# Keys times values of two pairs of heads in one slice, transposes apart from their loads, and another order of the first product's seven outer products

## The chip, the cores and the metric

One core of one Trainium2 chip runs the kernel. The metric is the time on the device in microseconds of one execution; smaller is better. PE is TensorE (the matrix engine), DVE is VectorE, ACT is ScalarE, POOL is GpSimd, SP is SyncE, whose queue issues nearly all DMAs here.

## What is computed

```python
kv  = einsum('bhsd,bhse->bhde', k, v)          # 8 batches, 8 heads, 576 rows, head size 64
out = einsum('bhsd,bhde->bhse', q, kv)         # linear attention, no softmax
rms = sqrt(mean(out * out, axis=-1, keepdims=True) + 1e-06)
x   = (out / rms * g_norm), heads side by side # 4608 rows x 512
h   = x @ w_in                                 # 512 -> 2048
g   = maximum(h, 0.0) ** 2
y   = g @ w_out                                # 2048 -> 512
```

All of it is in float32.

## The kernel before

The 4608 rows of x are 36 tiles of 128 rows, and four tiles make a strip: nine strips, numbered 0 to 8. A batch has 576 rows, four and a half tiles; the halves of two batches share a tile, so an even batch brings four tiles of its own, an odd one five, the first of them the shared one ("rest").

**The strips.** Each strip has an up part (x times `w_in`, then relu and square) and a down part (times `w_out`). Both use fast matrix multiplication: seven products of sums of blocks instead of eight of blocks. Strip 0 has an ordinary up part and one level in its down part; strip 1 has one level up and two levels down; strips 2 to 8 have two levels in both, 49 small products in each part. In those strips the up part is a list of 55 slots. `UP_SETS` orders the seven outer products ("sets", numbered 1 to 7): the set at place n issues its seven small products at slots 7n, 7n+2, ... 7n+12, so neighbouring sets alternate. Each small product is eight recorded matmuls. Three PSUM banks A, B and C serve a set. Bank A takes the inner products 1, 6, 7 and 4 one after another: each is added onto what lies there, so its former content is first copied to a `snap` tile (L1088 by ACT, or L1083 by DVE with an addition), and PE waits for that read. Bank B does so for 5 and 3.

**Where the sets' results go.** `UP_TO` names for each set the quarter of g that it writes and the quarter that it is added to: 11, 12, 21 and 22. Set 5 updates two quarters, and sends six of its additions to POOL (L1083). Four sets finish a quarter (`FINAL`): for these, relu and square run on ACT, in place (L1023, L1024), two or four slots after the product. DVE then makes the sums that the down part needs (`leaf_sums`, `add_s1`).

**POOL's sums.** The sets multiply `w_in` by four sums of x (`sum_x` 5, 6, 7 and 4) and by the inner sums of each set (`leaf_x`). POOL makes them at slots given by `SUM_AT` and by `at == 2`; those of the first set come at the end of the down part before (L966).

**Attention as slices.** Attention for the next strip is a list of slices that is worked off between the slots: `attend` spreads a strip's slices evenly over the first 42% of its weighted steps, so that they end near slot 46. Their kinds, in the order of a batch b from 2 on: for each of four pairs of heads `key_value` (20 recorded matmuls, two small copies on ACT, then the loads of keys and values two pairs ahead) and `transposed_query` (a DVE transpose, then the loads of queries two pairs ahead, four DMAs); after these, for each two tiles, `query` (64 recorded matmuls, squares on ACT), `mean_roots` (means on DVE, square root on ACT), `normalized` (reciprocal, a Newton step and a product on DVE), `squares_x` (DVE transposes), `send_x` (a store) and, later, `fetch_x` (four loads that turn the tile into x transposed). Keys, values and queries have two buffers each. Batches 0 and 1 use PE for the transposes (`features`, L527) instead of the store and loads. In strip 0 the slices follow a formula of their own (L1195 to L1197).

Each engine works through its instructions in the order written; the order is written by hand.

Of the kernel before, what the change touches and what calls it, by code (L numbers as in the profile page):

```python
# [10 lines left out]
FP32 = mybir.dt.float32  # L11
# [9 lines left out]
def kernel(  # L21
# [285 lines left out]
    ident = const.tile([P, P], FP32, name="ident")  # L307
    make_identity(nc, ident)

    kv_all = const.tile([P, 2 * NP + 1, P], FP32, name="kv_all")  # L310
    nc.gpsimd.memset(kv_all, 0.0)
    nc.vector.memset(k_rest, 0.0)
    nc.vector.memset(v_rest, 0.0)
# [26 lines left out]
    def keep_busy(ps, n):  # L340


        for _ in range(n):
            nc.tensor.matmul(ps, lhsT=ident, rhs=ident[:, : ps.shape[1]], start=True, stop=True)
# [25 lines left out]
            nc.tensor.transpose(ps[:, p], flat(q_rest[b // 2][:, 2 * p : 2 * p + 2]), ident)  # L370
        nc.scalar.copy(open_rest(b), ps)

    def key_value(b, p):
        tk, tv = main.pop(("k", b, p)), main.pop(("v", b, p))

        ps = apsum.tile([P, D], FP32, name="kv_ps", tag="at")
        if (b, p) == (0, 0):
            keep_busy(ps, 3)
        for c in range(C + 1):
            for h in range(2):  # L380
                a, w = (tk[:, h, c, :], tv[:, h, c, :]) if c < C else (k_rest[:, 2 * p + h], v_rest[:, b % 2, 2 * p + h])
                nc.tensor.matmul(ps[ts(h, D)], lhsT=a, rhs=w, start=c == 0, stop=c == C)  # L382
        d = kv_all[:, (NP * b + p) % (2 * NP + 1)]
        nc.scalar.copy(d[0:D, 0:D], ps[0:D])
        nc.scalar.copy(d[D:P, D:P], ps[D:P])
        kvd[b, p] = d
        if b < 2:
            if b == 1 and p < 2:
                load_next()
        else:  # L390
            load_next(names="kv")
            if p == NP - 1 and b + 1 < B:
                load_rest(b + 1, nc.sync)

    by_head = lambda t: t.rearrange("p (h d) -> p h d", d=D)

# [49 lines left out]

    queried = []

    def query(ns):
        ps = products_x(ns)  # L450
        parts = [ps[:, :, i] for i in range(len(ns))]
        queried.append((parts, squared_parts(parts)))

    def mean_roots(ns):
        parts, sqs = queried.pop()
# [135 lines left out]
    for b in range(1, B):  # L591
        for p in range(NP):
            pair = [(transposed_query, (b, p)), (key_value, (b, p))]
            slices += pair if b < Q_ON_PE else pair[::-1]
            fetch(1)
            if (b, p) == (X_ON_PE, 0):
                slices += late
        if b % 2 and b < Q_ON_PE:
            slices.append((rest_queries, (b,)))
        first_n = b // 2 * PAIR + (C if b % 2 else 0)  # L600
        ns = list(range(first_n, first_n + C + b % 2))
        for i in range(0, len(ns), 2):
            pair = ns[i : i + 2]
            slices += [(query, (pair,)), (mean_roots, (pair,))]
            fetch(1)
            slices.append((normalized, (pair,)))
            fetch(1)
            for n in pair:
                if b < X_ON_PE and i == C:

                    late = [(features, (n,))]
                    continue
                slices.append((features if b < X_ON_PE else squares_x, (n,)))
                if b < X_ON_PE and n % NT == NT - 1:
                    ready[n // NT] = len(slices)
            if b >= X_ON_PE:
                slices += [(send_x, (n,)) for n in pair]
                fetches.extend(pair)
    fetch(2)
    slice_at = [0]  # L620

# [119 lines left out]
    for p, t in zip((1, 2, 5), w_first):  # L741
        w_blk[0, p] = t.rearrange("p f (h e) -> p h f e", h=2)
    DEEP_ORDER = (4, 1, 2, 6, 5, 7, 3)
    UP_SETS = (1, 2, 6, 7, 5, 3, 4)
    to_stream = [(s, p) for s in range(DEEP) for p in ORDER if (s, p) not in w_blk]
    for s in range(DEEP, N_STRIP):
        to_stream += [("in", s, p) for p in UP_SETS if s >= DEEP_UP]
# [172 lines left out]
    def down_deep(s, k, i):  # L920
        p = DEEP_ORDER[k]
        if s == N_STRIP - 1 and k == 6 and i == 1:

            steps = together(s, p)
            for js in ((1,), (2, 6, 5, 7), (4, 3)):
                small_products(s, p, js)
                next(steps)
            return
        if k == 0 and s >= DEEP_UP:
            if i == 0:  # L930
                return
            for j in (7, 5, 6, 3):
                small_products(s, p, (j,))
                if first_sums_g:
                    first_sums_g.pop(0)()
            stream(2)
            leaf_sums(s, DEEP_ORDER[1])
            for slot in sorted(relus):
                relu_squares(slot)
            for slot in sorted(first_s):  # L940
                add_s1(s, slot)
            return
        if k == 6 and i == 1:
            small_products(s, p, (4,))
            return
        if s < N_STRIP - 1 or k < 6:
            small_products(s, p, ((1, 2, 3), (4, 5, 6, 7))[i])
        stream()
        q11, q12, q21, q22 = (gq[s, q] for q in (11, 12, 21, 22))
        if i == 1:  # L950
            if k == 3:
                minus(nc.vector, q22, q22, q11)
            if k == 4:
                minus(nc.vector, q21, q21, q11)
            if k == 6:
                deque(together(s, p), 0)
            return
        if k == 2:
            minus(nc.vector, q11, q12, q11)
        if k == 3:  # L960
            leaf_sums(s, DEEP_ORDER[k + 1])
        if k:
            deque(together(s, DEEP_ORDER[k - 1]), 0)
        if k < 6 and k != 3:
            leaf_sums(s, DEEP_ORDER[k + 1])
        if k == 6 and s + 1 < N_STRIP:  # L966
            leaf_x(s + 1, 0)


    first_s = {}  # L970
# [52 lines left out]
            nc.scalar.activation(o, o, AF.Relu)  # L1023
            nc.scalar.activation(o, o, AF.Square)  # L1024

    SUM_AT = {2: 5, 4: 6, 11: 7, 18: 4}
    FINAL = (2, 5, 3, 4)
    UP_TO = {1: (12, None), 2: (11, 12), 6: (12, 12), 7: (21, 12), 5: (22, 21), 3: (12, 12), 4: (21, 21)}
    up_bank = {}

    def up_slot(s, slot):

        for n, p in enumerate(UP_SETS):
            i, odd = divmod(slot - 7 * n, 2)
            if not odd and 0 <= i < 7:
                up_small(s, n, p, ORDER[i], slot)
        if slot in SUM_AT:
            sum_x(s, SUM_AT[slot])
        n, at = divmod(slot, 7)
        if at == 2 and n < 6:  # L1040
            leaf_x(s, n + 1)
        if s == DEEP_UP and at == 0 and n < 7:
            deep_differences_in(A_IN[UP_SETS[n]])
        relu_squares(slot)
        add_s1(s, slot)
        if slot in (1, 3, 5):
            small_products(s - 1, 3, ((slot + 9) // 2,))
        if slot == 5:
            stream()
            deque(together(s - 1, 3), 0)  # L1050
        if slot == 45:
            first_sums_g[:] = leaf_sums(s, 4, (3, 1, 2, 4))
        if slot in (49, 51, 53):
            small_products(s, 4, ({49: 1, 51: 2, 53: 4}[slot],))
        if slot in (46, 48, 50, 52):
            first_sums_g.pop(0)()

    def up_small(s, n, p, j, slot):
# [62 lines left out]
    for s in range(N_STRIP):  # L1121
# [21 lines left out]
        for i, (w, fn, a) in enumerate(steps):  # L1143
# [87 lines left out]
```

## Time and profile before

| | us |
|---|---|
| five runs: median (lowest to highest) | 968.47 (958.34 to 972.83) |
| the profiled execution | 968.47 |
| its span | 966.7 |
| mean granted PE clock | 0.974 |

Where the strips lie in the span: strip 0 down from about 95 to 164 us, strip 1 up to 230 and down to about 273. Then, for strips 2 to 8, the up part: 273 to 332, 372 to 434, 475 to 535, 575 to 637, 677 to 742, 782 to 832, 872 to 921. What lies between is the down part, about 40 us each, and the last one ends at 966.

A group in the profile is a source line, an engine, an operation and its tiles (`out<-in`); "idle before" is the time that an engine stood before such an instruction, and the arrow names what released it. Matmul ends are modelled, so a busy PE may still run slowly; the granted clock shows that.

The units of the sums below, in mean ns of one instruction: relu 627 and square 631 (128x512), `snap` copy on ACT 583, POOL's addition for set 5 1328, DVE's stream transpose 701, the small ACT copies of `key_value` (64x64) 203 and 207, squares of one tile on ACT 593.

### The profile page before, as it was taken

The page shows a single profiled execution, that of the slowest core. Times are in us where ns is not written, and L with a number is a line of the kernel's source. Part 1 is how long each engine was busy: PE and PEld are TensorE (multiplying, and loading weights), DVE is VectorE, ACT ScalarE, POOL GpSimd, SP SyncE. Part 2 cuts the span into 40 slices and gives each one's busy share as a digit, 9 for nine tenths or more (in the row PEclk, how much of TensorE's full clock was granted, in tenths as well). Part 3 has the DMA queues.
Part 4 walks back from the last instruction along what each step waited for, and adds up shares of the span by engine and source line. Part 5 has one row for each costly group of instructions (what it writes and reads, how often), then busy time and mean ns, then how long its engine had stood idle before and what let it go on. Part 6 is the DMA issues. An engine that isn't in the chain of part 4 may idle for free.

```text
span 966.7 us, 20798 instructions
## 1 busy us (share of the span) xinstructions
PE 902.7 (93%) x8246; PEld 838.2 (87%) x8246; DVE 755.2 (78%) x1289; ACT 323.2 (33%) x662; POOL 265.5 (27%) x287
## 2 busy tenths in 40 slices
PE   6999779899999899889998999889988999999997
PEld 6434668679999899889997999889988999999997
DVE  3899947688958897589768977699658977895696
ACT  3797223221024602361145114440325024403520
POOL 0000000252056404250345033503332056124600
PEclk8999989899999999999999999999989999999999
DMA  9699987678887587858888887788755876685385
GB/s 277 208 281 321 291 308 219 175 220 299 331 233 222 187 327 258 218 172 305 276 217 217 296 289 226 164 287 313 216 150 176 322 233 197 227 311 175 139 294 175
DMA packets 173809, 235.73 MB, mean 244 GB/s; under 512 B 85008, under 2 KB 138768, under 8 KB 165264
## 3 DMA queue, kind: packets, MB, share of 16 engines
q1 hardware_dynamic: 173392, 234.27, 75.4%
q8 instruction: 65, 1.06, 0.4%
q14 instruction: 32, 0.26, 0.1%
q10 hardware_dynamic: 320, 0.13, 0.1%
HBM read 197.66 MB, written 36.70 MB: 242 GB/s over the span
## 4 chain that ended last, share of the span: by engine, by line
PE 63%; DVE 16%; DMA 8%; ACT 4%; SPq 3%; issue 3%; POOL 3%; DVEq 0%; POOLq 0%; ACTq 0%
PE ps_B L888 19%; PE ps_A L888 15%; PE ps_A L1071 12%; PE ps_B L1071 6%; PE ps_C L1071 3%; PE ps_A L667 3%; POOL gt L1083 2%; DVE ms L429 2%; DMA w_blk<-w_deep 2%; PE ps_B L667 2%; PE kv_ps L382 1%; DVE w_c L242 1%; DVE gt L1083 1%; DVE snap L1083 1%; DMA v<-in_v_dram 1%
## 5 line engine op out<-in xcount | busy, mean ns | idle before, releaser
L888 PE MATMUL ps_B<-w_blk,g_s 128*128 128x128 f32 x1024 | 126.0, 275 | 0.0
L888 PEld LDWEIGHTS ps_B<-w_blk,g_s 128*128 128x128 f32 x1024 | 120.0, 192 | 0.0
L1071 PE MATMUL ps_A<-x_l,w_in 128*128 128x128 f32 x784 | 108.1, 282 | 11.0 <-ACT snap L1088 10.7
L1071 PEld LDWEIGHTS ps_A<-x_l,w_in 128*128 128x128 f32 x784 | 97.3, 195 | 13.3 <-ACT snap L1088 8.4
L888 PE MATMUL ps_B<-w_blk,gt 128*128 128x128 f32 x768 | 98.5, 277 | 0.0
L888 PE MATMUL ps_A<-w_blk,g_s 128*128 128x128 f32 x768 | 93.6, 275 | 0.0
L888 PEld LDWEIGHTS ps_B<-w_blk,gt 128*128 128x128 f32 x768 | 92.8, 194 | 0.1
L888 PEld LDWEIGHTS ps_A<-w_blk,g_s 128*128 128x128 f32 x768 | 89.6, 192 | 0.0
L262 POOL TENSOR_TENSOR x_l<-xT 128x256 f32<-128x256 f32 x21 | 17.0, 809 | 255.2 <-PE ps_A L888 215.9
L1023 ACT ACTIVATE gt<-gt 128x512 f32<-128x512 f32 x112 | 70.2, 627 | 40.5 <-DVE gt L1083 21.8
L1083 POOL TENSOR_TENSOR snap<-snap,gt 128x512 f32<-128x512 f32 x35 | 45.2, 1292 | 136.5 <-ACT snap L1088 110.2
L1088 ACT COPY snap<-ps_A 128x512 f32<-128x512 f32 x63 | 36.7, 583 | 132.8 <-PE ps_A L1071 120.4
L888 PE MATMUL ps_A<-w_blk,gt 128*128 128x128 f32 x576 | 72.3, 275 | 0.2 <-DMA w_blk<-w_deep 0.2
L1024 ACT ACTIVATE gt<-gt 128x512 f32<-128x512 f32 x112 | 70.6, 631 | 3.6
L1083 POOL TENSOR_TENSOR gt<-gt,snap 128x512 f32<-128x512 f32 x42 | 54.9, 1328 | 57.8 <-DVE snap L1083 57.8
L888 PEld LDWEIGHTS ps_A<-w_blk,gt 128*128 128x128 f32 x576 | 68.2, 192 | 0.4 <-DMA w_blk<-w_deep 0.4
L983 POOL TENSOR_TENSOR w_i<-w_in 128x512 f32<-128x512 f32 x7 | 10.3, 1467 | 191.9 <-DMA v<-in_v_dram 164.7
L903 DVE TENSOR_TENSOR o_sb<-o_sb,ps_B 128x256 f32<-128x256 f32 (+1 forms) x128 | 49.3, 385 | 16.5 <-ACT o_sb L904 9.0
L262 DVE TENSOR_TENSOR gt<-gt 128x2048 f32<-128x2048 f32 (+1 forms) x29 | 59.6, 2062 | 0.0
L1071 PE MATMUL ps_A<-x_l,w_blk 128*128 128x128 f32 x392 | 52.4, 277 | 4.0 <-POOL snap L1083 3.4
L904 ACT COPY o_sb<-ps_A 128x128 f32<-128x128 f32 x24 | 6.4, 265 | 145.7 <-PE ps_A L888 145.7
L1071 PE MATMUL ps_B<-x_l,w_blk 128*128 128x128 f32 x392 | 53.4, 280 | 0.0
(171 smaller groups left out, 1823.2 us busy)
## 6 DMA issues: line engine op xcount, KB each, us to landing
w_blk<-w_deep SPq DMA_DIRECT2D x56, 1024.0 KB, 6.3
w_blk<-w_out SPq DMA_DIRECT2D x56, 768.0 KB, 5.6
w_blk<-w_in_deep SPq DMA_DIRECT2D x49, 768.0 KB, 5.4
raw<-in_moe_w_in_dram SPq DMA_DIRECT2D x16, 512.0 KB, 6.0
raw<-in_moe_w_out_dram SPq DMA_DIRECT2D x16, 512.0 KB, 5.8
k<-in_k_dram SPq DMA_DIRECT2D x29, 256.0 KB, 4.3
v<-in_v_dram SPq DMA_DIRECT2D x29, 256.0 KB, 4.5
x_d<-x_q SPq DMA_DIRECT2D x27, 256.0 KB, 5.5
```

The lines of the kernel that those rows point to most:

```text
L242: yield nc.vector.scalar_tensor_tensor(out=ci, in0=high, scalar=-(2**30), in1=ci, op0=ALU.bitwise_and, op1=ALU.bitwise_or)
L262: eng.tensor_tensor(out=out, in0=a, in1=b, op=ALU.subtract)
L429: nc.vector.reduce_sum(out=ms[:, i], in_=by_head(sq), axis=AX.X)
L667: nc.tensor.matmul(bank[BANK[p]][:, i, :], lhsT=lhsT(k), rhs=rhs(k), start=p in (1, 5, 2) and i == 0 and k == 0, stop=k == n - 1, skip_gro ...
L888: nc.tensor.matmul(chain[c][x][:, i, :], lhsT=a[:, f, :], rhs=w[:, f, :], start=x not in opened[c] and f == 0, stop=f == FQ // 2 - 1, skip ...
L903: add = lambda out, a, b: nc.vector.tensor_tensor(out=out, in0=a, in1=b, op=ALU.add)
L983: nc.gpsimd.tensor_tensor(out=s1, in0=w_half(b, 0, 1), in1=w_half(b, 1, 1), op=ALU.add)
L1023: nc.scalar.activation(o, o, AF.Relu)
L1024: nc.scalar.activation(o, o, AF.Square)
L1071: nc.tensor.matmul(ps[:, i, :], lhsT=w, rhs=rhs, start=j in (1, 2, 5) and i == 0, stop=True, skip_group_check=True)
L1083: add = lambda eng, out, a, b: eng.tensor_tensor(out=out, in0=a, in1=b, op=ALU.add)
L1088: nc.scalar.copy(t, ps)
```

## The change

- `key_value` takes one or two pairs of heads. For two, their products share one PSUM tile, and two copies on ACT (64 partitions, two times 64 columns) take the place of four. Loads for both follow the copies. `kv_all` has eight slots instead of nine.
- From batch 2 on `key_value` is no slice of its own: `query` of the first and second two tiles of batch b calls it for two pairs each of batch b+1, between its products and its squares. Batch 2 itself gets two slices of two pairs.
- `transposed_query` of batch b+1 is put one by one before the `squares_x` slices of batch b (`turn`), with what is left before the next batch's first query.
- In batch 1 `query_means` takes the means to the query, and `roots_normalized` takes the root and the normalization to one slice. Four slices per two tiles instead of five.
- The list of slices is 210 long instead of 235.
- `UP_SETS` is 1, 6, 7, 5, 2, 3, 4 instead of 1, 2, 6, 7, 5, 3, 4; set 1 now writes quarter 11, set 6 adds to it and writes 12, set 2 adds onto 11 and finishes it.
- POOL makes sums 5 and 6 and the inner sums of the second set at the end of the down part before; sums 7 and 4 come at slots 6 and 20.
- The first sums of the down part start at slot 40 instead of 45.
- Strip 1's seven groups of weight sums on POOL come in another order of blocks.

```diff
-    def key_value(b, p):
-        tk, tv = main.pop(("k", b, p)), main.pop(("v", b, p))
-        ps = apsum.tile([P, D], FP32, name="kv_ps", tag="at")
...
-        d = kv_all[:, (NP * b + p) % (2 * NP + 1)]
-        nc.scalar.copy(d[0:D, 0:D], ps[0:D])
-        nc.scalar.copy(d[D:P, D:P], ps[D:P])
...
+    def key_value(b, *ps_of):
+        ps = apsum.tile([P, len(ps_of), D], FP32, name="kv_ps", tag="at")
+        for i, p in enumerate(ps_of):
+            tk, tv = main.pop(("k", b, p)), main.pop(("v", b, p))
...
+                    nc.tensor.matmul(ps[ts(h, D), i], lhsT=a, rhs=w, start=c == 0, stop=c == C)
+        at = (NP * b + ps_of[0]) % (2 * NP)
+        d = kv_all[:, at : at + len(ps_of)]
+        nc.scalar.copy(d[0:D, :, 0:D], ps[0:D])
+        nc.scalar.copy(d[D:P, :, D:P], ps[D:P])
+        for i, p in enumerate(ps_of):
+            kvd[b, p] = d[:, i]
...
+                load_next(names="kv")
+                if p == NP - 1 and b + 1 < B:
+                    load_rest(b + 1, nc.sync)
...
+    def query(ns, *keys):
         ps = products_x(ns)
+        if keys:
+            key_value(*keys)
         parts = [ps[:, :, i] for i in range(len(ns))]
         queried.append((parts, squared_parts(parts)))
+
+    def query_means(ns):
+        query(ns)
+        parts, sqs = queried.pop()
+        queried.append((parts, mean_of(sqs)))
+
+    def roots_normalized(ns):
+        parts, ms = queried.pop()
+        queried.append((parts, (ms, root_of(ms))))
+        normalized(ns)
...
+    for pair in query_pairs(1):
+        slices += [(query_means, (pair,)), (roots_normalized, (pair,))]
...
+    slices += [(key_value, (2, 0, 1)), (transposed_query, (2, 0))] + late + [(transposed_query, (2, 1))]
+    slices.append((key_value, (2, 2, 3)))
+    ahead = deque((transposed_query, (2, p)) for p in (2, 3))
+
+    def turn():
+        if ahead:
+            slices.append(ahead.popleft())
+
+    for b in range(2, B):
+        for i, pair in enumerate(query_pairs(b)):
+            while i == 0 and ahead:
+                turn()
+            slices.append((query, (pair, *((b + 1, 2 * i, 2 * i + 1) if i < 2 and b + 1 < B else ()))))
+            slices.append((mean_roots, (pair,)))
             fetch(1)
             slices.append((normalized, (pair,)))
             fetch(1)
+            if i == (2 if b % 2 else 1) and b + 1 < B:
+                ahead.extend((transposed_query, (b + 1, p)) for p in range(NP))
             for n in pair:
+                turn()
+                slices.append((squares_x, (n,)))
+            slices += [(send_x, (n,)) for n in pair]
+            fetches.extend(pair)
...
-    UP_SETS = (1, 2, 6, 7, 5, 3, 4)
+    UP_SETS = (1, 6, 7, 5, 2, 3, 4)
...
         if k == 6 and s + 1 < N_STRIP:
             leaf_x(s + 1, 0)
+            sum_x(s + 1, 5)
+            sum_x(s + 1, 6)
+            leaf_x(s + 1, 1)
...
-    SUM_AT = {2: 5, 4: 6, 11: 7, 18: 4}
+    SUM_AT = {6: 7, 20: 4}
...
-    UP_TO = {1: (12, None), 2: (11, 12), 6: (12, 12), 7: (21, 12), 5: (22, 21), 3: (12, 12), 4: (21, 21)}
+    UP_TO = {1: (11, None), 2: (11, 11), 6: (12, 11), 7: (21, 12), 5: (22, 21), 3: (12, 12), 4: (21, 21)}
...
-        if at == 2 and n < 6:
+        if at == 2 and 0 < n < 6:
             leaf_x(s, n + 1)
...
-        if slot == 45:
+        if slot == 40:
             first_sums_g[:] = leaf_sums(s, 4, (3, 1, 2, 4))
...
-        if slot in (46, 48, 50, 52):
+        if slot in (41, 43, 45, 47):
             first_sums_g.pop(0)()
...
-                    deep_sums_in(i // 3 - 2)
+                    deep_sums_in((1, 6, 5, 4, 0, 2, 3)[i // 3 - 2])
```

More of the change, by code (lines that the diff above doesn't have):

```diff
@@ L308 @@
     make_identity(nc, ident)
-    kv_all = const.tile([P, 2 * NP + 1, P], FP32, name="kv_all")
+    kv_all = const.tile([P, 2 * NP, P], FP32, name="kv_all")
     nc.gpsimd.memset(kv_all, 0.0)
@@ L371, in rest_queries @@
         nc.scalar.copy(open_rest(b), ps)
-    def key_value(b, p):
-        tk, tv = main.pop(("k", b, p)), main.pop(("v", b, p))
-        ps = apsum.tile([P, D], FP32, name="kv_ps", tag="at")
[L377 to L382, printed above, removed]
-        d = kv_all[:, (NP * b + p) % (2 * NP + 1)]
-        nc.scalar.copy(d[0:D, 0:D], ps[0:D])
-        nc.scalar.copy(d[D:P, D:P], ps[D:P])
[L386 to L393, printed above, removed]
+    def key_value(b, *ps_of):
+        ps = apsum.tile([P, len(ps_of), D], FP32, name="kv_ps", tag="at")
+        for i, p in enumerate(ps_of):
+            tk, tv = main.pop(("k", b, p)), main.pop(("v", b, p))
+            if (b, p) == (0, 0):
+                keep_busy(ps[:, 0], 3)
+            for c in range(C + 1):
+                for h in range(2):
+                    a, w = (tk[:, h, c, :], tv[:, h, c, :]) if c < C else (k_rest[:, 2 * p + h], v_rest[:, b % 2, 2 * p + h])
+                    nc.tensor.matmul(ps[ts(h, D), i], lhsT=a, rhs=w, start=c == 0, stop=c == C)
[5 more added lines that the diff above has]
+            kvd[b, p] = d[:, i]
+            if b < 2:
+                if b == 1 and p < 2:
+                    load_next()
+            else:
+                load_next(names="kv")
+                if p == NP - 1 and b + 1 < B:
+                    load_rest(b + 1, nc.sync)
     by_head = lambda t: t.rearrange("p (h d) -> p h d", d=D)
@@ L447 @@
     queried = []
-    def query(ns):
+    def query(ns, *keys):
         ps = products_x(ns)
+        if keys:
+            key_value(*keys)
         parts = [ps[:, :, i] for i in range(len(ns))]
         queried.append((parts, squared_parts(parts)))
+    def query_means(ns):
[6 more added lines that the diff above has]
+        normalized(ns)
     def mean_roots(ns):
@@ L589, in fetch, with query_pairs @@
                 ready[n // NT] = len(slices)
[L591 to L599, printed above, removed]
+    def query_pairs(b):
         first_n = b // 2 * PAIR + (C if b % 2 else 0)
         ns = list(range(first_n, first_n + C + b % 2))
-        for i in range(0, len(ns), 2):
-            pair = ns[i : i + 2]
-            slices += [(query, (pair,)), (mean_roots, (pair,))]
+        return [ns[i : i + 2] for i in range(0, len(ns), 2)]
+    for p in range(NP):
+        slices += [(transposed_query, (1, p)), (key_value, (1, p))]
+    slices.append((rest_queries, (1,)))
+    for pair in query_pairs(1):
+        slices += [(query_means, (pair,)), (roots_normalized, (pair,))]
+        for n in pair:
+            if n == PAIR - 1:
+                late = [(features, (n,))]
+                continue
+            slices.append((features, (n,)))
+            if n % NT == NT - 1:
+                ready[n // NT] = len(slices)
+    slices += [(key_value, (2, 0, 1)), (transposed_query, (2, 0))] + late + [(transposed_query, (2, 1))]
[10 more added lines that the diff above has]
+            slices.append((mean_roots, (pair,)))
             fetch(1)
@@ L607 @@
             fetch(1)
+            if i == (2 if b % 2 else 1) and b + 1 < B:
+                ahead.extend((transposed_query, (b + 1, p)) for p in range(NP))
             for n in pair:
[L609 to L618, printed above, removed]
+                turn()
+                slices.append((squares_x, (n,)))
+            slices += [(send_x, (n,)) for n in pair]
+            fetches.extend(pair)
     fetch(2)
```

## The prediction

> **What bounds the kernel now.** I read the page from the top, then TensorE's waits, then busy time by stretch, then the timeline around each wait. The page's first part:
>
> ```profile
> PE 902.7 (93%) x8246; PEld 838.2 (87%) x8246; DVE 755.2 (78%) x1289; ACT 323.2 (33%) x662; POOL 265.5 (27%) x287
> ```
>
> TensorE is busy for 93% of the span, so at most 64 us are idle. But busy time also grows when the clock is halved. By stretch (start:end, length, then busy us of PE, PEld, DVE, ACT, POOL, then clock, DMA share, GB/s):
>
> ```profile
> 677.00:742.00 65.00, 58.06 (x636) 56.61 (x635) 42.41 (x73) 27.57 (x56) 24.35 (x28) 0.92 0.56 169
> ...
> 742.00:782.00 40.00, 40.00 (x361) 40.00 (x360) 34.88 (x56) 4.08 (x11) 8.03 (x10) 1.00 0.85 306
> ...
> 872.00:921.00 49.00, 48.34 (x432) 48.03 (x431) 32.29 (x49) 22.91 (x41) 24.15 (x28) 1.00 0.45 153
> ```
>
> Down parts (742:782) have no gap. Up parts with attention take 59 to 65 us (273, 372, 475, 575, 677), the last one without it 49. Attention's own matmuls are 5.3 to 6.5 us of each, so some 35 us over five strips are neither: stops and slow clock. The waits name them (total, times, longest):
>
> ```profile
> PE ps_A L1071 <- ACT snap L1088: 10.7, 5, 3.1
> PE xt_ps L527 <- DVE x_n L467: 9.2, 2, 4.8
> PE kv_ps L382 <- DMA v<-in_v_dram: 7.3, 4, 3.9
> PE ps_A L667 <- ACT snap L677: 5.6, 3, 3.6
> ...
> PE ps_B L1071 <- DVE snap L1083: 4.2, 4, 1.7
> ...
> PE ps_A L1071 <- POOL snap L1083: 3.4, 2, 1.9
> ...
> PE x_ps L412 <- DVE qT L350: 2.2, 1, 2.2
> ```
>
> These are the places that the diff touches. The longest of two kinds, with the cause of the second, in the strip that starts at 677:
>
> ```profile
> 706.25 1.12 PE L382 MATMUL kv_ps<-v,k 128*64 128x64 f32 x16 [3.87 <-DMA v<-in_v_dram]
> ...
> 707.51 2.08 PE L1071 MATMUL ps_B<-x_l,w_blk 128*128 128x128 f32 x8
> ...
> 727.07 2.50 POOL L1083 TENSOR_TENSOR gt<-gt,snap 128x512 f32<-128x512 f32 x2
> ...
> 729.60 0.63 ACT L1023 ACTIVATE gt<-gt 128x512 f32<-128x512 f32 x1 [3.25 <-POOL gt L1083]
> ...
> 735.42 0.57 ACT L1088 COPY snap<-ps_A 128x512 f32<-128x512 f32 x1
> ...
> 736.04 2.08 PE L1071 MATMUL ps_A<-x_l,w_in 128*128 128x128 f32 x8 [3.07 <-ACT snap L1088]
> ```
>
> Set 5 sends six additions to POOL. A relu on ACT waits 3.25 us for one of them, and the copy of bank A stands behind that relu and the following ones, so PE stops. Eight matmuls after a long stop take 2.08 us instead of 1.06.
>
> **The skill.** "TensorE: Matmul & The Clock Gate", What's actually happening: an idle window of about 3.4 us halves the clock. The 2.08 us agree; so a stop of 3 us costs nearer 5. "SBUF — State Buffer", Who interferes with whom: a VectorE instruction with two SBUF inputs and a GpSimd instruction that reads SBUF exclude each other for a whole instruction. The trace agrees: the 128x16 product L443, 0.18 us elsewhere, took 1.19 us at 307.69 beside POOL's additions. "Perfetto Trace Analysis", Sequencer Loop: each engine's instructions wait for semaphores in its queue; the relu that holds the copy shows it.
>
> **The change, part by part.** Positions are up-part slots (0.893 us of PE each, eight matmuls) or steps of strip 1 (1.73 to 1.93 us); I walked both slice lists through the pacing by hand.
>
> *A. Strip 0, normalization at the query.* Before, `normalized` and `features` come in one step, and PE waits 4.83 and 4.37 us for DVE. After, the normalization is issued two steps before its transposes: VectorE has the means at 111.6, needs 0.3 for ACT's root, 0.8 for four small operations and 1.29 for two products, so it ends near 114.2, and PE arrives at 115.2. For the second pair, squares end at 129.1 and DVE idles until 137 (12.22 us before L273); it ends near 132, and PE needs it near 135. The 9.2 us go, and slow matmuls behind them (5.40 and 5.07 us for 16, 3.62 elsewhere: 3.2; transposes 1.3): 13.7 at most. The four-instruction order on ACT is unchanged. Next late are `sums_in`, held until 137.6 by the landing of `w_out<-w_in` (issued to 127.4, 10.2 us), and the last weight block of strip 0 (issued 135.06): PE would need both near 143, so I take **10**, bounds 4 and 13.7.
>
> *B. Strip 1.* At 167 POOL's first `deep_sums_in` reads block 0, already there, and three DVE operations of `sums_in` take 4.99 us instead of 2.0; the root and then the copy are late, and PE stops 3.6 us at 176.48 and runs slow (3.78 and 2.72 us where 1.9 is usual: 2.7). Starting with block 1, the last one DVE writes, keeps POOL off until DVE is through; means also come a step earlier. Of 6.3 us I take **+4**. Against that, two pairs of keys free and refill both buffers at once: the loads for batch 3 are issued at step 5 and used at step 7. Four issues of 0.45 us, two of the rest's of 0.65, 4.7 to landing: 7.8 us, against 6.3 (two steps, 1.1 of query, 1.5 of products). The fourth query load of batch 2 is issued at step 4 and wanted at 6: four issues (2.8) after others and 4.2 to land against some 5.3. Stops of 1.5 to 2 and slow clock: **-3**. Bounds of B -8 and +6.
>
> *C. Keys from DMA.* In strips 3, 5, 6 the waits of 2.5, 0.6 and 3.9 us and the slow matmuls after them (1.8 and 2.6, excess over the usual records) make 11.4. After, each double load has 14 slots (12 us) or more before its use against about 7 needed, so all go, except that SP's queue may hold one: **10**, bounds 5 and 11.4. SP issues the same DMAs; a rest load goes with the second group, a strip before its use.
>
> *D. Query loads.* Transposes are now moved apart, some bunched: strip 3 has them at slots 6, 13, 15, 17 and the query at 19; strip 5 at 17, 23, 25, 26 and 28. The load for the fourth starts when the second has freed its buffer: 0.7 + 2.6 of four issues + 4.2 to land + 0.7 = 8.2 us, against 5.4 and 4.5 until the query, less 0.8 of products that come first in both. VectorE stands there, with the set's additions and ACT's relus behind it; PE stops 2 to 3.5 us, and slow clock of 1 after each: 8, less the present 2.2: **-6**, bounds -12 and +2.
>
> *E. Order of sets.* Set 5 comes one set earlier and set 2, now final, between it and set 3, so nothing adds to POOL's results at once; leaf sums start five slots earlier. At stake in strips 2 to 8: ACT 10.7, DVE 4.2 + 0.7 + 0.3, POOL 3.4, and slow matmuls (some 3): 22. But four final sets now follow each other. One costs ACT eight relu/squares (0.63) and a copy (0.58), 5.6 us of the 6.25 that PE gives; a query there costs ACT 1.4. So ACT stays nearly full, and its 3.25 us wait moves to slot 35, still able to stop PE at 43 or 50, by 1 to 2 us: **+11**, bounds -5 and 20.
>
> *F. Copies on ACT.* Twelve groups: four of 0.205 become two of about 0.265 (the nearest row, L904's 128 columns): 0.29 each, 3.5 us of ACT, which is not at its limit then: **+0.5**; without that cover 3.5. Copies stand before squares now and wait 1.5 us for the products; PE makes nothing for ACT meanwhile.
>
> *G. POOL's sums in the down part.* Two sums (1.3 each) and a leaf (1.7) per strip move into a part where DVE is 92% busy and excluded by them. The cover is PE's queue of two banks; if it is gone, up to 2 us per strip. I take **-2** over seven strips, bounds -8 and 0. The smaller `kv_all` costs nothing: its ring is read before it is written, in the same slice.
>
> Sum: 10 + 4 - 3 + 10 - 6 + 11 + 0.5 - 2 = 24.5. The profiled execution took 968.47 us (span 966.7, 1.8 around it), which is the median of the five shown. 968.5 - 24.5 = **944**.
>
> **Rivals.** *The stops only move* (0.16). For it: ACT's nearly full half, and DMA shares above 1.0 from 120 to 140 that may hold strip 0. Against it: TensorE has room at every place. E = 0, A = 4, the rest as above: 4 + 1 + 10 - 6 - 1.5 = 7.5, so 961; with D at its bound 967.
>
> *VectorE stands for query loads* (0.13, slower). The place: the fourth transposes of strips 3 and 5 and steps 6 and 7 of strip 1. SP's queue is in order, and it already waited up to 4.6 us for one x store and 8.7 for a weight buffer; if such a wait falls before a load, a stop is 6.5 us and 2.5 of slow clock, 9 each, 36 for four. The gains with E at 0 and A, C as taken are 22, so 968.5 + 14 = 982. It decides from some 6 us per stop. Against it: the present kernel's seven-slot leads had one 2.2 us stop.
>
> *It doesn't do what it says* (0.01): the waits stay with the same releasers; 968.
>
> **The numbers.** Forecast 0.70, own range 933 to 955. Within 1% (958.8 to 978.2) is about what a measurement can't tell from no change. Faster by more 0.71, within 0.16, slower 0.13. The range 931 to 967 takes in the first rival and leaves the second out.
>
> **What would show it.** Right: no PE wait on `x_n` before 150; no wait on `v` after 270; strip 6's up part near 55 us with clock above 0.97; ACT's waits for POOL near slot 35, with PE stops under 2 us. Wrong: `qT` waits above 5 us in strips 3 and 5 (D); PE waits on `snap` still above 8 us in sum (E); down parts above 41 us (G); strip 0 ending later than 158 (A). The forecast fails outright if gaps on PE after 270 still add up to 25 us.

## The result and the profile after

| | us |
|---|---|
| kernel before, median (lowest to highest) | 967.25 (957.01 to 975.03) |
| changed kernel, median (lowest to highest) | 965.24 (959.5 to 970.32) |
| ratio, 95% interval | 0.9995 (0.9981 to 1.0008) |
| span of the profiled executions, before and after | 966.7 and 966.3 |

The change makes no measurable difference; 944 was forecast. The first part of the changed kernel's page has nearly the same load on every engine, ACT 3.5 us and POOL 4.6 us less:

```profile
PE 901.7 (93%) x8246; PEld 839.5 (87%) x8246; DVE 754.6 (78%) x1289; ACT 319.7 (33%) x638; POOL 260.9 (27%) x287
```

A total that stands still can hide large moves, so I cut both spans at the same products:

| stretch | before | after | difference |
|---|---|---|---|
| strip 0 down | 72.0 | 59.9 | -12.1 |
| strip 1 up | 65.8 | 80.3 | +14.5 |
| strip 1 down | 40.9 | 46.1 | +5.2 |
| up parts of strips 2 to 8, sum | 419.8 | 412.6 | -7.2 |
| down parts of strips 2 to 7, each | 38.2 to 38.7 | 38.2 to 38.4 | 0 |

So 19 us are won and 20 lost. TensorE's waits in the changed kernel (total, times, longest) name the places. Line numbers are 28 to 31 higher than before in the later part: L1102 was L1071, L1114 was L1083, L1119 was L1088.

```profile
PE ps_B L1102 <- DVE snap L1114: 7.9, 7, 1.9
PE kv_ps L382 <- DMA v<-in_v_dram: 7.6, 4, 4.1
PE x_ps L414 <- DVE qT L350: 5.5, 2, 3.8
PE x_ps L414 <- DVE qT_rest L352: 5.2, 3, 3.5
...
PE ps_A L1102 <- ACT snap L1119: 4.2, 6, 1.6
PE ps_A L1102 <- POOL x_l L262: 3.4, 2, 2.8
PE ps_A L916 <- DMA w_blk<-w_out: 3.3, 1, 3.3
...
PE ps_A L1102 <- issue: 2.7, 5, 1.2
...
PE ps_A L1102 <- DVE gt L1114: 1.6, 1, 1.6
```

The waits for `x_n` are down from 9.2 us to 2.2, and ACT's `snap` costs 4.2 in place of 10.7. In their place stand VectorE's `snap` (7.9, was 4.2), POOL's `x_l`, queries (10.7, were 2.5) and a weight block. Values cost 7.6 us (7.3 before), all four waits now before 205 us. The five lines of L1102, the products of the sets, add to 19.8 us; those of L1071 in the kernel before add to 19.8 as well. So the change has moved these stops about and not lessened them. The window that was worst before, strip 6's up part (66.84 us), and the last one:

```profile
679.35:741.15 61.80, 55.67 (x572) 54.41 (x571) 45.98 (x77) 26.31 (x48) 25.20 (x30) 0.94 0.57 167
...
869.87:920.61 50.74, 50.07 (x444) 49.53 (x443) 32.06 (x50) 23.92 (x42) 25.25 (x30) 1.00 0.44 151
```

Strip 6 is 5 us shorter, but its clock is 0.94 and 6 us of gaps are left. The last strip, which has no attention, has only the new order of sets to feel, and is no faster (50.4 before).

### The profile page after: what moved, and what is told of

Read it like the earlier page. It is cut to its first block, busy times and chain, and to the rows that moved or that the text cites. A ratio compares the mean times of both kernels' runs of the same rounds, so it can differ in the third digit from the quotient of the medians.

```text
span 966.3 us, 20794 instructions
## 1 busy us (share of the span) xinstructions
PE 901.7 (93%) x8246; PEld 839.5 (87%) x8246; DVE 754.6 (78%) x1289; ACT 319.7 (33%) x638; POOL 260.9 (27%) x287
## 4 chain that ended last, share of the span: by engine, by line
PE 59%; DVE 17%; DMA 8%; ACT 4%; SPq 4%; POOL 4%; issue 4%; DVEq 0%; POOLq 0%; ACTq 0%
PE ps_B L916 19%; PE ps_A L916 16%; PE ps_A L1102 10%; PE ps_B L1102 5%; POOL gt L1114 3%; PE ps_C L1102 2%; DVE gt L1114 2%; DMA v<-in_v_dram 2%; PE ps_A L695 2%; DMA q<-in_q_dram 2%; DVE snap L1114 2%; DVE g_s L262 1%; DVE w_c L242 1%; PE kv_ps L382 1%; SPq L121 1%
## 5 line engine op out<-in xcount | busy, mean ns | idle before, releaser
L1102 PE MATMUL ps_A<-x_l,w_in 128*128 128x128 f32 x784 | 106.8, 280 | 4.9 <-ACT snap L1119 4.2
L1102 PEld LDWEIGHTS ps_A<-x_l,w_in 128*128 128x128 f32 x784 | 97.3, 195 | 6.9 <-ACT snap L1119 4.5
L1119 ACT COPY snap<-ps_A 128x512 f32<-128x512 f32 x63 | 36.6, 581 | 151.1 <-PE ps_A L1102 138.0
L1114 POOL TENSOR_TENSOR snap<-snap,gt 128x512 f32<-128x512 f32 x35 | 46.0, 1315 | 132.1 <-ACT snap L1119 90.8
L1114 POOL TENSOR_TENSOR gt<-gt,snap 128x512 f32<-128x512 f32 x42 | 52.6, 1273 | 51.2 <-DVE snap L1114 51.2
L1102 PE MATMUL ps_A<-x_l,w_blk 128*128 128x128 f32 x392 | 53.3, 280 | 5.5 <-POOL x_l L262 2.8
L1102 PEld LDWEIGHTS ps_A<-x_l,w_blk 128*128 128x128 f32 x392 | 48.5, 195 | 6.5 <-issue 3.5
```

Source lines behind the costliest of these rows:

```text
L1102: nc.tensor.matmul(ps[:, i, :], lhsT=w, rhs=rhs, start=j in (1, 2, 5) and i == 0, stop=True, skip_group_check=True)
L1114: add = lambda eng, out, a, b: eng.tensor_tensor(out=out, in0=a, in1=b, op=ALU.add)
L1119: nc.scalar.copy(t, ps)
```

## Experiments

"Ratio" (the second number of each result) is against the kernel before, with a 95% interval; 0.01 is 9.7 us. Ratios carry the scatter of the kernel before too: two kernels of 954.06 and 954.26 us below have 0.9898 and 0.9858, so less than 4 us between two ratios says little. Every kernel's span was cut as in the table above. Such lengths come from one profiled execution each: strip 0's down part, for one, took 57.1 to 62.8 us in the kernels that have batch 1's new slices.

### Parts put alone into the kernel before

**Batch 1's slices** (A):

```diff
-            slices += [(query, (pair,)), (mean_roots, (pair,))]
...
+            if b < X_ON_PE:
+                slices += [(query_means, (pair,)), (roots_normalized, (pair,))]
```

> The kernel before with batch 1's slices alone changed (means to the query, root and normalization in one slice). Theory 1 (the gain in strip 0 is real, and other parts of the change give it back in strip 1): PE's waits for x_n before 150 us go, strip 1's products start some 11 us earlier, its up part stays near 66 us, and the run is 9 to 12 us below the kernel before, near 957. Rival (the gain of strip 0 is only borrowed: strip 1 then waits for weights, loads or POOL's sums that come no sooner): strip 1's up part grows to 75 us or more and the time stays at 964 or above.

Measured 959.74, ratio 0.9902 (0.9868 to 0.9937): 9.5 us. Strip 0 down takes 60.2 us. Strip 1 up takes 70.1, 4.3 more than before, because one wait of strip 0 comes again there:

```profile
PE xt_ps L537 <- DVE x_n L477: 7.8, 1, 7.8
```

Theory 1 holds for the larger part of the gain; the rival's share is those 4 us.

**The deep sums' order** (first half of B):

```diff
-                    deep_sums_in(i // 3 - 2)
+                    deep_sums_in((1, 6, 5, 4, 0, 2, 3)[i // 3 - 2])
```

> The kernel before with strip 1's seven weight sums on POOL in the new order of blocks alone. Forecast's term: PE's stop of 3.6 us near 176 us and the slow records after it go, 4 us less. Rival (the stop is hidden anyway or moves to the next step): within 1.5 us of the kernel before.

965.45, 0.9961 (0.9937 to 0.9985): 3.8 us, the size forecast. The 3.6 us stop is gone and strip 1 up takes 60.7; its down part takes 43.5, since a weight block is now 2.3 us late.

**The order of the sets, with POOL's sums and the leaf sums** (E and G):

```diff
-    UP_SETS = (1, 2, 6, 7, 5, 3, 4)
+    UP_SETS = (1, 6, 7, 5, 2, 3, 4)
...
-    SUM_AT = {2: 5, 4: 6, 11: 7, 18: 4}
+    SUM_AT = {6: 7, 20: 4}
...
-        if slot == 45:
+        if slot == 40:
```

> The kernel before with the order of the seven sets, POOL's sums and the first sums of the down part changed, attention as before. Theory 1 (the stops moved from ACT's snap to DVE's and the gain is small): PE's waits for snap in strips 2 to 8 fall from 20 to 17 or so and the time is 2 to 4 us below the kernel before. Rival, the forecast's own terms E and G: 9 us below, near 958. Second rival (POOL's sums in the down part cost): slower by 3 us or more, down parts above 41 us.

973.72, 1.0050 (1.0029 to 1.0072): 5 us slower. The second rival had the direction right, but not the place: the up parts of strips 2 to 8 add to 424.2 (419.8 before), while the down parts stay at 38.2, so it isn't the sums in the down part. VectorE's `snap` stopped PE for 14.0 us in place of 4.5, ACT's for 2.8 in the up sets in place of 10.7.

**A and the deep sums' order together**, both edits as above:

> The kernel before with two parts of the change alone: batch 1's slices and the order of the deep sums. If the two add up: 9.5 + 3.8 = 13.3 us below the kernel before, near 954.5, with strip 1's up part near 61 us. If they free the same waits of VectorE in strip 1: 957 to 960. If the first part's gain was partly held by the 7.8 us wait for x_n that the second part removes: 951 or less.

957.99, 0.9919 (0.9889 to 0.9948), about 8 us: less than the two added. A 5.6 us wait for `x_n` in strip 1 stayed. With the weight blocks asked for earlier as well:

```diff
-                if s == 1 and i == n_up - 2:
+                if s == 1 and i == n_up - 6:
                     stream(2)
```

> As the kernel with batch 1's slices and the deep sums' order alone, with strip 1's two streamed weight blocks asked for four steps earlier. If the late w_blk<-w_out (2.3 us where the deep sums' order alone was changed) is the queue's order: strip 1's down part falls from 43.5 to 41 us and the run is 2 us below the kernel without this edit. If it is the buffer that comes free late: no change, or POOL's sums wait longer.

959.84, 0.9952 (0.9921 to 0.9983): no gain; strip 1's down part took 43.4 us where it was 41.7 without the edit. In the kernel without the edit the block was only 0.5 us late, so the run says little about the 2.3 us above; that small item stays open.

### What makes strip 1 longer

A stop in the changed kernel's strip 1, in its timeline (start, length, engine, line):

```profile
168.90 5.81 SPq L121 DMA_DIRECT2D q<-in_q_dram  x6
169.60 0.70 DVE L350 STREAM_TRANSPOSE qT<-q 128x512 f32<-128x512 f32 x1
...
172.86 1.12 PE L382 MATMUL kv_ps<-v,k 128*64 128x64 f32 x16 [4.09 <-DMA v<-in_v_dram]
```

The keys and values of batch 2's next pairs were asked for from 165.98 to 168.34, behind which SP issues queries of several pairs in a row, and PE stands 4.09 us for those values. These loads were late already: SP had stood 5.7 us, to 165.07, for the landing of `w_deep<-w_t`, before it came to them in the order written. I first took the stop for the short lead of batch 2's double loads.

```diff
-    slices += [(key_value, (2, 0, 1)), (transposed_query, (2, 0))] + late + [(transposed_query, (2, 1))]
-    slices.append((key_value, (2, 2, 3)))
-    ahead = deque((transposed_query, (2, p)) for p in (2, 3))
+    slices += [(key_value, (2, 0)), (transposed_query, (2, 0))] + late
+    for p in range(1, NP):
+        slices += [(key_value, (2, p)), (transposed_query, (2, p))]
+    ahead = deque()
```

> The changed kernel with batch 2's keys and queries one pair at a time, as before, so that strip 1 holds 18 slices' work in the old spacing and later batches stay in pairs. Theory 1 (strip 1 loses what strip 0 wins because two pairs free and refill both buffers just before their next use): the waits for v of 7.6 us and DVE's 6.2 us for q in strip 1 fall below 2, its up part from 80 to about 70 us, and the run is 8 to 11 us below the changed kernel, near 956. Rival (strip 1 is held by something else): less than 3 us gained, 962 or above.

966.73, 0.9992 (0.9971 to 1.0014): nothing. The waits for `v` fell to 0.9 us, but `v_rest` took 5.7 and `x_n` 4.7, and strip 1 up was 82.3 us. Theory 1's reason fell.

Second theory: SP's queue. In strip 1 it issues 99 DMAs, 69 before. Half of the query loads of these slices go to ACT's queue:

```diff
-                    eng.dma_start(
+                    e = nc.scalar if a % 2 and (2, 2) <= (b, p) < (4, 2) else eng
+                    e.dma_start(
```

> The changed kernel with half of the query loads of strip 1 (two of the four DMAs of each, 20 in all) issued by ACT's queue in place of SP's. Theory 2 (SP's queue sets strip 1: it issues 99 DMAs in 68 of its 80 us, so loads land late wherever they stand): waits for v, v_rest and q in strip 1 fall by half or more, its up part from 80 to 73 us or less, the late w_blk<-w_out after it goes, and the run is 6 us or more below the changed kernel, 960 or less. Rival (the loads are late for their buffers, not for the queue, or ACT is held by the transposes that free them): within 2 us of the changed kernel, or slower, with ACT's snap copies late.

964.73, 1.0003 (0.9982 to 1.0024): nothing, strip 1 up 85.8 us, waits for `v` 9.8. "DMA: Bandwidth & Descriptors", Issuing engines are not separate DMA queues, says that all issuers share the same 16 engines and that a second one saves only issue time. The missing gain fits that, but the run doesn't clear the queue: SP now stood 16.5 us in strip 1 for query loads, where in the changed kernel it stood for none, so what it saved in issuing it lost in waiting.

The transfers come next. One line of the DMA view of strip 1's up part, of the kernel before and of the changed one:

```profile
DMA packets 22061, 14.35 MB, mean 218 GB/s; under 512 B 15492, under 2 KB 20504, under 8 KB 21800
```

```profile
DMA packets 31947, 18.11 MB, mean 225 GB/s; under 512 B 24080, under 2 KB 30224, under 8 KB 31622
```

The slice order pulls all of batch 3's keys and transposes, the first of its three queries and half of batch 4's keys into strip 1: 45% more packets, nearly nine tenths of the added ones under 512 B. The changed kernel by stretch (length, PE, PEld, DVE, ACT, POOL, clock, share of the DMA engines, GB/s):

```profile
167.91:183.91 16.00, 9.83 (x140) 7.98 (x139) 5.66 (x7) 2.33 (x5) 1.23 (x1) 0.79 0.99 255
183.91:191.91 8.00, 7.46 (x47) 6.55 (x48) 2.75 (x5) 1.67 (x5) 0.00 (x0) 0.79 0.41 62
191.91:207.91 16.00, 13.54 (x146) 11.07 (x146) 11.00 (x22) 4.74 (x11) 8.66 (x6) 0.89 1.00 337
```

For 32 of these 40 us the engines are full, and PE's clock is below 0.9. The middle row, where all packets are under 512 B, shows why bytes mislead: a share of 0.41 for 62 GB/s, so an estimated 150 at full share, where strip 1's down part moves 326 GB/s at 0.91. The same page, Specifications, asks for 512 B or more at full rate; this agrees.

Third theory, then: batch 3's work must leave strip 1. On top of the former order of sets (see below) and of batch 2 one pair at a time (as in the first of these runs), keys go to the query from batch 3 on only:

```diff
+        if b == 3:
+            for p in range(NP):
+                slices += [(key_value, (b, p)), (transposed_query, (b, p))]
+                fetch(1)
...
-            slices.append((query, (pair, *((b + 1, 2 * i, 2 * i + 1) if i < 2 and b + 1 < B else ()))))
+            slices.append((query, (pair, *((b + 1, 2 * i, 2 * i + 1) if i < 2 and 2 < b and b + 1 < B else ()))))
...
-            if i == (2 if b % 2 else 1) and b + 1 < B:
+            if i == (2 if b % 2 else 1) and 2 < b and b + 1 < B:
```

> The changed kernel with the former order of sets and with keys in the query only from batch 3 on: batch 3's keys, queries and transposes go back behind batch 2, out of strip 1. Theory 3 (strip 1 is held by its transfers: 32,000 packets in place of 22,000, engines at a share of 1.0 for 30 of its 80 us, so every load is late whoever issues it): strip 1's up part falls from 82 to 62 to 68 us, some 5 us of work go to strip 2, the late w_blk after it goes, and the run is 6 to 10 us below the kernel with the former order alone, 944 to 948. Rival (strip 1 is held by its stops for the first features and for weights, whatever the loads): less than 3 us gained, 951 or above.

959.38, 0.9911 (0.9883 to 0.9939), some 5 us above the two kernels below that have the former order alone (954.06 and 954.26; the ratios are 1 and 5 us apart). Strip 1 up fell from 81.9 to 72.1 and its down part from 45.0 to 41.2, as theory 3 says, but strip 2 rose from 53.3 to 73.8: PE waited 7.9 us for `v_rest`, since batch 4's first keys now follow batch 3's last within some 6 us, and one load of the rest lies between them. Calling them one query later:

```diff
-            slices.append((query, (pair, *((b + 1, 2 * i, 2 * i + 1) if i < 2 and 2 < b and b + 1 < B else ()))))
+            slices.append((query, (pair, *((b + 1, 2 * (i - (b == 3)), 2 * (i - (b == 3)) + 1) if b > 2 and 0 <= i - (b == 3) < 2 and b + 1 < B else ()))))
```

> As the kernel with keys in the query from batch 3 on, but batch 3 calls them from its second and third query in place of its first and second, so that the rest of batch 4's values has a query's time more to land (it waited 7.9 us in strip 2, and strip 2 grew to 73.8 us). Theory 3 (strip 1 is held by its transfers; the loss in strip 2 was this one load): strip 1 stays near 72 us and its down part at 41, strip 2 falls to 62 to 65 us, the run is 8 to 11 us lower than that kernel and 3 to 5 below the one with the former order alone, 948 to 951. Rival (the transfers taken out of strip 1 are late wherever they stand): strip 2 stays at 70 or more, 956 or above.

947.88, 0.9798 (0.9756 to 0.9841). Strip 1 up takes 65.9 us, strip 2 takes 63.6, and the line answers to the two above:

```profile
DMA packets 21986, 15.63 MB, mean 237 GB/s; under 512 B 15472, under 2 KB 20236, under 8 KB 21644
```

Strip 1 with its down part is 18.7 us shorter than with the former order alone (15 in the two kernels below that keep this placement), and strip 2 10.3 longer. So at least half of strip 1's growth was work that had moved (100 matmuls of keys and 64 of queries more than before, with their transposes), and some 5 to 8 us were loss. That batch 3's slices in strip 1 cause the loss is shown. How they do so is not shown. That they fill the engines is a guess, which the mean shares don't bear out. Here is strip 1 up of this kernel and of the one with the former order alone, in the same columns as above:

```profile
154.12:219.98 65.86, 59.45 (x491) 49.21 (x490) 47.54 (x73) 18.54 (x39) 28.38 (x21) 0.97 0.80 237
```

```profile
149.14:231.07 81.93, 69.82 (x655) 58.72 (x654) 51.67 (x82) 20.22 (x42) 29.49 (x21) 0.90 0.82 227
```

The engines are as full in the shorter strip (0.80 and 0.82). SP's queue, where a load stands behind whatever SP waits for, is the rival that no run settles.

**The features of tile 8 two pairs later**, with a last wait in mind:

```diff
-    slices += [(key_value, (2, 0)), (transposed_query, (2, 0))] + late
-    for p in range(1, NP):
-        slices += [(key_value, (2, p)), (transposed_query, (2, p))]
+    for p in range(NP):
+        slices += [(key_value, (2, p)), (transposed_query, (2, p))] + (late if p == 2 else [])
```

> As the kernel before it in this list, with the transposes of strip 1's last own tile (features of tile 8) after the third pair of batch 2 in place of the first. If PE's wait of 5.3 us for x_n in strip 1 is only too early a place in PE's order: it goes with the slow records behind it, strip 1's up part falls from 72 to 65 us or less, 5 to 8 us lower. Rival (PE then waits at the next step for VectorE's additions, which stand behind the same sums): 2 us lower or less.

947.15, 0.9786 (0.9741 to 0.9831): the rival. The wait for `x_n` went, and one of 5.6 us for `v` came in its place.

### The sets' order: which half of it costs

**The former order in the changed kernel:**

```diff
-    UP_SETS = (1, 6, 7, 5, 2, 3, 4)
+    UP_SETS = (1, 2, 6, 7, 5, 3, 4)
...
-        if slot == 40:
+        if slot == 45:
```

> The changed kernel with the former order of the seven sets, POOL's sums and leaf sums. If the parts are independent, the order costs here what it cost alone, 4.8 us: near 962, 4 to 6 us below the changed kernel, with PE's waits for snap of DVE (7.9 us) mostly back at ACT. Rival (the new order pays once keys and transposes are moved, since fewer copies stand on ACT then): 966 or above.

954.06, 0.9898 (0.9855 to 0.9940): some 10 us faster than the changed kernel. The up parts of strips 2 to 8 add to 399.1, from 412.6. All waits of the products of the sets in this kernel:

```profile
PE ps_A L1099 <- ACT snap L1116: 7.2, 6, 2.3
...
PE ps_B L1099 <- DVE snap L1111: 2.7, 4, 1.3
```

They add to 9.9 us, against 19.8 in the changed kernel. Of those 19.8 only 12.1 are waits for `snap`, so counting `snap` alone would have shown 2 us of the 10.

**The new order, with the leaf sums late:**

```diff
-        if slot == 40:
+        if slot == 45:
...
-        if slot in (41, 43, 45, 47):
+        if slot in (46, 48, 50, 52):
```

> The changed kernel with the first sums of the down part (four subtractions and additions on VectorE for set 4's operand) back at slots 45 to 52, the new order of sets kept. If the early sums are what costs (they stand on VectorE among set 2's and set 3's additions, with bank B's snap behind them): PE's waits for DVE's snap (7.9 us) fall below 4 and the run is 5 to 10 us below the changed kernel. Rival (the order itself costs: set 2's additions fall beside POOL's work for set 5): within 2 us of the changed kernel, or the sums are late for the down part and its first products wait.

955.15, 0.9871 (0.9848 to 0.9894), up parts 400.9, waits of the products of the sets 11.8 us. So the whole loss hangs on five slots of the leaf sums, and the new order with late sums is worth nothing either way in this kernel: its waits for `snap` are 6.4 us against 9.9 with the former order, but 3.5 for POOL's `x_l` and 1.6 for `gt` come in their place. The former order with early sums was not run. VectorE in strip 4 of the changed kernel:

```profile
533.05 0.68 DVE L262 TENSOR_TENSOR g_s<-g_s,gt 128x512 f32<-128x512 f32 x1
533.65 0.68 DVE L1114 TENSOR_TENSOR gt<-ps_A,gt 128x512 f32<-128x512 f32 x1
534.25 0.68 DVE L1006 TENSOR_TENSOR gt<-gt 128x512 f32<-128x512 f32 x1
534.85 0.68 DVE L262 TENSOR_TENSOR g_s<-gt,g_s 128x512 f32<-128x512 f32 x1
535.45 0.68 DVE L1114 TENSOR_TENSOR snap<-ps_B,gt 128x512 f32<-128x512 f32 x1
```

And PE's product that waits for this `snap`, first in the timeline of the changed kernel, then in that of the kernel with the late sums:

```profile
536.19 1.05 PE L1102 MATMUL ps_B<-x_t,w_blk 128*128 128x128 f32 x7 [1.86 <-DVE snap L1114]
```

```profile
527.67 1.16 PE L1102 MATMUL ps_B<-x_t,w_blk 128*128 128x128 f32 x8 [0.66 <-DVE snap L1114]
```

VectorE has no idle time in these rows. The last of them empties bank B. In the changed kernel all four leaf sums (`g_s`; the others at 527.35 and 529.15) lie ahead of it at 0.6 us each from start to start, in the other kernel one does, and PE stands 1.2 us longer. Nothing but the down part's products wants these sums.

**POOL's sums in the down part** (G), with the former order:

```diff
+            sum_x(s + 1, 5)
+            sum_x(s + 1, 6)
+            leaf_x(s + 1, 1)
...
-    SUM_AT = {2: 5, 4: 6, 11: 7, 18: 4}
+    SUM_AT = {11: 7, 18: 4}
...
-        if at == 2 and n < 6:
+        if at == 2 and 0 < n < 6:
```

> The changed kernel with the former order of sets and leaf sums, but POOL's sums 5 and 6 and the second set's inner sums kept at the end of the down part before. Forecast's term G (they hold VectorE in the down part): 1 to 4 us slower than without them there, down parts above 38.2 us. Rival (the down part has two banks of slack, and the up part's first slots lose POOL work): within 1.5 us of it, 953 to 956, down parts at 38.2.

954.26, 0.9858 (0.9827 to 0.9889), down parts 38.2: the same as without them. With the former order G costs nothing, and PE doesn't wait for `x_l`. Whether G or the order brings those 3.5 us in the kernel with late sums, no run shows.

### The queries, and a version that beats both

On top of the kernel with tile 8's features later, the transposes begin behind the last query of the batch before:

```diff
+            if i == (2 if b % 2 else 1) and 2 < b and b + 1 < B:
+                ahead.extend((transposed_query, (b + 1, p)) for p in range(NP))
+                turn()
             slices.append((mean_roots, (pair,)))
             fetch(1)
+            if len(pair) == 1:
+                turn()
             slices.append((normalized, (pair,)))
             fetch(1)
-            if i == (2 if b % 2 else 1) and 2 < b and b + 1 < B:
-                ahead.extend((transposed_query, (b + 1, p)) for p in range(NP))
```

> As the kernel before it in this list, with each batch's transposes from batch 4 on begun right after the last query of the batch before (one after it, one after the means where the last pair is one tile), in place of in a row before the next query. Forecast's term D (bunched transposes stop PE in strips 3 and 5 because the fourth load of queries comes late): waits for qT and qT_rest of 8 to 10 us fall to 3 or less, 5 to 9 us lower. Rival (the loads are late for the queue and the engines, and earlier transposes push them into other loads): waits for v or v_rest come in their place, within 2 us.

936.05, 0.9678 (0.9640 to 0.9715): 11 us faster than without the edit and 3.2% faster than the kernel before. PE's waits of its profile from the top:

```profile
PE ps_A L1106 <- ACT snap L1123: 6.5, 5, 2.0
PE kv_ps L382 <- DMA v<-in_v_dram: 5.9, 1, 5.9
PE x_ps L491 <- ACT kv_all L386: 4.9, 4, 3.0
PE ps_A L1106 <- issue: 4.4, 4, 1.8
```

`qT` and `qT_rest` have left the top (0.5 us together), no up part from strip 2 on has a clock below 1.00, and strip 6 takes 54.4 us.

## Why the prediction was wrong

**E is the step that failed.** It put +11 on the order of sets, and listed "leaf sums start five slots earlier" among the gains, at no price. The early sums cost 10 us in the changed kernel; without them the order gives about 0. The stops at ACT's and POOL's `snap` did shrink as E said (from 14.1 us to 4.2), but VectorE's `snap`, `gt`, POOL's `x_l` and small waits of PE's own took their place, 19.8 us in all before and after. With the former order the changed kernel takes 954, and the forecast without E and G is 953; that this fits so well is in part luck, as the terms below show errors that cancel. The prediction saw ACT full in the second half of the up part and looked for what would come late behind it there; VectorE's rows in those slots were as dense, and the change puts four instructions among them earlier. Its stake was too large as well: of the 18.6 us of waits for `snap`, the six kernels with keys moved and the former order have 9.1 to 13.9 left, so moving the keys had already taken 5 to 9 of what E counted.

**A** was right: +10 forecast, 9.5 alone, strip 0 ends at 151.9, and of the waits for `x_n` before 150 only 0.4 us are left, which the kernel before has too. **B**'s first half, +4, was right alone (3.8), but A and it together gave 8 to 10, not 14: probably both draw on VectorE's backlog at the start of strip 1, which the 5.6 us wait for `x_n` there suggests. B's second half, -3 for two short leads, was mis-sized: strip 1 with its down part grew by 20 us, of which some 10 come back in strip 2 with the work, so the loss is 5 to 8. The step counted the loads of batch 2 and the first of batch 3, and not what the new list holds of batches 3 and 4. The place that the second rival named, a wait of SP ahead of a load in strip 1, did come (5.7 us, and PE's stop of 4.09), but not at the size that it needed.

**C** was right in kind: no wait for values after 205. **D** was right in place (3.8 us in strip 3, 1.7 in strip 5) and too small: it left out `qT_rest` in strips 4 and 6 (1.2 and 3.5 us), and spreading the transposes brought 11 where 6 was set, near its lower bound of 12. C, D, F and B's second half together were put at +1.5; the kernel with former order against the one with A and the deep sums alone gives 2 to 4, with larger losses in B and D than set, and with 5 to 9 us of waits for `snap` gone that the forecast had under E. F's copies take 0.26 us each and ACT's busy time fell by 3.5 us, both as estimated; no run isolates what that is worth. **G**, -2, is 0 with the former order.

The marks set beforehand said so: strip 6's up part takes 61.8 us at a clock of 0.94, not near 55 above 0.97; waits on `snap` of 12.1 us, above 8, condemn E; `qT` at 5.5, above 5, D; down parts at 38.2 clear G; and gaps after 270 us add to 30 (412.6 less 382.5 of busy PE), above the 25 named for outright failure. The first rival, *the stops only move*, with E at 0, gave 961 and came nearest, by luck in part: its E was still too good, and its A of 4 was less than half of the 9.5 measured.

## What to carry to other kernels

Price every instruction that is moved earlier, on the engine that runs it, also when it is moved out of a harmless place: a sum wanted late and issued early stands ahead of work wanted now. Add up all waits of a product, whatever they are put down to; those for one tile can fall while the sum stays. When a list of work is paced by its length, compare what each stage holds of it before and after, in transfers and packets too; a stage can lose what the one before it wins. Where parts of a change point both ways, measuring each alone finds the version that neither end shows, here 3.2%.

## What was not expected of the hardware

With half of strip 1's query loads on ACT's queue, SP stood 16.5 us there for loads of queries, and nothing was won. Where all packets were under 512 B the DMA engines were 0.41 busy for 62 GB/s, by proportion an estimated 150 at full share, against an estimated 358 with large ones (326 at 0.91). Strips 2, 4, 7 and 8 of the changed kernel kept a clock of 1.00 with stops for `snap` of up to 1.9 us; short as they are, the early sums made PE's waits in seven strips 8 us longer (19.8 against 11.8). Of the prediction's "idle window of about 3.4 us" the traces show the halved clock and not the length: in the kernel before, a stop of 3.07 us was followed by eight matmuls in 2.08 us, one of 2.87 us, ended at 631.53, by eight in 1.16.
